# Linear attention and a mixture of experts in one kernel: the queries' sums by head move from TensorE and spreading transfers to ScalarE and VectorE

## The chip, the cores and the metric

The kernel runs on one core of a Trainium2 chip. A core has TensorE (matrix products into PSUM), VectorE, ScalarE and GpSimd for work on tiles of 128 partitions, and queues that start DMA transfers (SP's, ScalarE's and GpSimd's). The time is that of the whole program on the device in microseconds, and is given as the median of several runs. All numbers are in fp32; most products are made as three products of a high and a low part.

## The reference

```
qkv = x @ wqkv                                   # S = 2048 tokens, D = 512; 32 heads of 16
phi = lambda t: where(t > 0, t + 1, exp(t)) + 1e-6
pq, pk = phi(q), phi(k)
kv  = einsum("bhsd,bhse->bhde", pk, v)
z   = einsum("bhsd->bhd", pk)                    # sum of the keys over all tokens, by head
num = einsum("bhqd,bhde->bhqe", pq, kv)
den = einsum("bhqd,bhd->bhq", pq, z)[..., None] + 1e-6
a   = (num / den) @ wo
b   = sum over 8 experts: softmax weight * (silu(x @ w1[e]) @ w2[e])     # F = 1792
g   = sigmoid((x * gate_w).sum(-1))
out = g * a + (1 - g) * b
```

What matters here is `den`: for each token and each of the 32 heads, the sum over the head's 16 features of query times `z`. The kernel divides the query by `den` and multiplies it by the gate `g` before the product with the folded matrix of `kv` and `wo`.

## The kernel before

**Staging.** A first stage (`keys`) makes the keys' features and their sums: `pks` is a tile whose sum over partitions is `z`. The second stage (`experts`) is one long loop over ticks, `for u in range(LAG + NTICK)`, with an order written out by hand. In each tick TensorE does six products "up" (`up`, `product`: hidden layers of a group of two blocks of F, by Strassen's seven products, into PSUM banks a, b and c) and six products "down" (`tick`: the second layer into four banks `p`, of the pool `dn`). A part is 49 ticks, seven phases P1, P7, P2, P4, P6, P5, P3 of seven ticks; it is one expert and one half of the tokens. The attention is two more parts of 14 ticks each, `A[0]` and `A[1]`. While the tick's products run, `other()` gives ScalarE and VectorE work for later ticks: `prep` splits weights into a high part (`o`, ScalarE) and a low part (`o`, VectorE), `high` and `low_h` do the same for hidden values (`ho`), `differ` forms differences of `s` tiles. At the end of a phase `evict` empties the `p` banks: in P2 VectorE multiplies the bank by the expert's weights (`finish`, tile `c`), then ScalarE copies `keep` (`k`) into the bank.

**The queries' sums.** The queries' features lie in DRAM (`pqd`) as four blocks of 128 features by 512 tokens for each of four token blocks i. `m.beside` names the four parts beside which they are worked on: the first two experts of the second half, and two experts after `A[0]`. Step s of query i stands in tick t0 + s of its part.

- In stage two's start, `normaliser` makes on TensorE, with 16 products of 32x32 against a tile of ones, the vector z for all features in 32 equal columns, masks it by head on VectorE (`maskh`) and stores it in `zcd`.
- `queries_load` (s = -3) loads the masked z (`Q.z`) once for two queries, and the four blocks `Q.d`, over SP's queue. All of them lie in two large buffers (tag `rm`), named `az` and `pq` in the profile.
- `queries_first`, s = 0 to 3: ScalarE adds EPS to the four blocks. `queries_last`, s = 3: TensorE makes `dn`, four fp32 products of the blocks with the masked z, in one bank of pool `a`: the sums by head. s = 4: ScalarE copies `dn` to `r`, and the gate's row is loaded over all partitions (`rg`). s = 5 to 8: VectorE takes the reciprocal, a quarter at a time. s = 9: VectorE multiplies by the gate, and GpSimd's queue stores 8 heads of each block in `rd`. s = 10: it loads them back, each head's row spread over the 16 partitions of its features (`az<-rd`). s = 15 to 18: VectorE multiplies the blocks by them, SP's queue stores them in `pqd`, and the fourth block is spread.
- `load_query` reads `pqd` for the attention's parts, 100 ticks and more later.

The engines take their instructions in order, and so do the queues; semaphores hold an instruction until its inputs are there and its buffer is free.

Of the kernel before, what the change touches and what calls it, by code (L numbers as in the profile page):

```python
# [16 lines left out]
P = 128  # L17
# [26 lines left out]
@with_exitstack  # L44
def gated_mix_kernel(ctx: ExitStack, tc: tile.TileContext, xT, x, wk, wv, wqkv_q, wo, wm, out):
    nc = tc.nc
    PS = bass.MemoryType.PSUM

    const = ctx.enter_context(tc.tile_pool(name="const", bufs=1))
    xpool = ctx.enter_context(tc.tile_pool(name="xpool", bufs=14))  # L50
    w1p = ctx.enter_context(tc.tile_pool(name="w1p", bufs=1))
    psum = ctx.enter_context(tc.tile_pool(name="psum", bufs=1, space=PS))
    dram = ctx.enter_context(tc.tile_pool(name="dram", bufs=1, space=bass.MemoryType.DRAM))
    ctx.enter_context(tc.manual_schedule())

    m = SimpleNamespace(nc=nc, tc=tc, const=const, xpool=xpool, w1p=w1p, psum=psum, v=nc.vector,
                        xT=xT, x=x, wk=wk, wv=wv, wq=wqkv_q, wo=wo, wm=wm, out=out)

    def mm3(ps, wh, wlo, xh, xl, start, stop):
        nc.tensor.matmul(ps, wh, xh, start=start, stop=False, skip_group_check=True)  # L60
        nc.tensor.matmul(ps, wh, xl, start=False, stop=False, skip_group_check=True)  # L61
        nc.tensor.matmul(ps, wlo, xh, start=False, stop=stop, skip_group_check=True)  # L62

    def act_copy(dst, src, scale=1.0, bias=0.0):
        nc.scalar.activation(dst, src, AF.Copy, scale=scale, bias=bias)  # L65

    def ps_tile(name, tag, bufs=None):
        return psum.tile([P, TB], F32, name=name, tag=tag, bufs=bufs or {"a": 2, "b": 1, "c": 1, "dn": 4}[tag])

    m.mm3, m.act_copy, m.ps_tile = mm3, act_copy, ps_tile  # L70


    def phi_first(dst, src):
        nc.scalar.activation(dst, src, AF.Exp)
        nc.scalar.activation(src, src, AF.Relu)

    def phi_last(dst, src):
        nc.vector.scalar_tensor_tensor(dst, dst, 1.0, src, op0=ALU.min, op1=ALU.add)

    def phi(dst, src):  # L80
        phi_first(dst, src)
        phi_last(dst, src)

    def eps_high(h, d):
        act_copy(h, d, bias=EPS)

    def eps_low(lo, d, h):
        nc.vector.scalar_tensor_tensor(lo, d, EPS, f32(h), op0=ALU.add, op1=ALU.subtract)

    m.phi, m.phi_first, m.phi_last, m.eps_high, m.eps_low = phi, phi_first, phi_last, eps_high, eps_low  # L90
    m.ident = const.tile([P, P], F32, name="ident")


    def x_tile(name, tag="x"):
        return xpool.tile([P, 2, TB], F32R, name=name, tag=tag, bufs=14 if tag == "x" else 2)

    m.x_tile = x_tile
    m.XO = [[None] * 7, [None] * 7]
    m.xstash = dram.tile([7, 2, P, 2 * TB], F32, name="xstash")
    m.w2stash = [dram.tile([P, 2, D], F32, name=f"w2stash{i}") for i in range(7 * (E * NPAIR + 2) // 2)]  # L100
    m.wgtd = dram.tile([E + 1, S], F32, name="wgtd")
    m.acct = dram.tile([2, 2, KT, P, TB], F32, name="acct")
    m.pqd = dram.tile([2, 2, KT, P, TB], F32, name="pqd")
    m.wpd = [dram.tile([P, D], F32, name=f"wpd{c}") for c in range(KT)]
    m.zcd = dram.tile([P, KT * NH], F32, name="zcd")
    m.rd = dram.tile([2, 2, NH, TB], F32, name="rd")

    X = [[SimpleNamespace(e=e, h=h, n=NPAIR) for e in range(E)] for h in range(2)]  # L110
    A = m.A = [SimpleNamespace(e=E, h=h, n=2) for h in range(2)]
    M = E // 2

    m.parts = [*X[0], *X[1][:M], A[0], *X[1][M:], A[1]]
    at = 0
    for part in m.parts:
        part.t0, at = at, at + 7 * part.n
    m.NTICK = at
    m.groups = [(part, q) for part in (A[0], *X[0], *X[1][:M], A[1], *X[1][M:]) for q in range(part.n)]
    m.NG = len(m.groups)  # L120
    for part in m.parts:
        part.gs = [g for g, (p, _) in enumerate(m.groups) if p is part]
    m.G1 = X[1][0].gs[0]

    m.beside = [*X[1][:2], *X[1][M:M + 2]]

    misc = ExitStack()
    m.misc = misc.enter_context(tc.tile_pool(name="misc", bufs=1, side="right"))


    def pad(pool):
        nc.gpsimd.memset(pool.tile([P, 24], F32, name="pad", tag="pad", bufs=1), 0.0)

    m.pad = pad
    weights(m)
    keys(m)
    experts(m, misc)


# [186 lines left out]
def keys(m):  # L326
# [31 lines left out]
        return X[tb, k // 2][c][:, k % 2, lo:hi]  # L358

    mask = m.mask = misc.tile([P, P], F32, name="mask")  # L360
    maskh = m.maskh = misc.tile([P, KT, NH], F32, name="maskh")
    pks = m.pks = misc.tile([P, D], F32, name="pks")
    ones = m.ones = misc.tile([P, NH], F32, name="ones")
    lg = m.lg = misc.tile([P, NT, NL], F32, name="lg")
# [83 lines left out]
    def bands(t):  # L448
        if t == 5:
            band(mask.rearrange("p (b e) -> p b e", e=DH), [[-DH, P // DH], [0, DH]], 1)  # L450
        elif t == 6:
            band(maskh, [[P, KT], [-DH, NH]], 1)

    pk = {}

# [130 lines left out]
def experts(m, misc):  # L586
# [335 lines left out]


    def normaliser():
        ps = ps_tile("z", "dn")[:, :KT * NH]
        for c in range(KT):
            for a in range(QT):
                nc.tensor.matmul(ps[a * SQ:(a + 1) * SQ, c * NH:(c + 1) * NH],
                                 m.pks[:, c * P + a * SQ:c * P + (a + 1) * SQ], m.ones, start=(c == 0), stop=True,
                                 skip_group_check=True)  # L930
        zf = r_tile("zf")[:, :KT * NH].rearrange("p (c f) -> p c f", c=KT)
        v.scalar_tensor_tensor(zf, ps.rearrange("p (c f) -> p c f", c=KT), S * EPS, m.maskh, op0=ALU.add, op1=ALU.mult)
        nc.sync.dma_start(m.zcd, zf.rearrange("p c f -> p (c f)"))

    def gates(step):
        g = m.lg[:, :, :E]
# [36 lines left out]

    Q = SimpleNamespace()

    def queries_load(i):
        if i % 2 == 0:
            az = m.raw_tile(f"az{i}")
            Q.z = az[:, :KT * NH].rearrange("p (c f) -> p c f", c=KT)
            Q.by = [az[:, KT * NH + c * TB:KT * NH + (c + 1) * TB] for c in (0, 1, 2, 0)]  # L980
            nc.sync.dma_start(az[:, :KT * NH], m.zcd)
        Q.d = m.raw_tile(f"pq{i}").rearrange("p (c t) -> p c t", c=KT)
        for c in range(KT):
            nc.sync.dma_start(Q.d[:, c], m.pqd[i // 2, i % 2, c])

    def queries_first(i, s):
        h, j = divmod(i, 2)

        def spread(c):
            heads = m.rd[h, j, c * P // DH:(c + 1) * P // DH]  # L990
            nc.gpsimd.dma_start(Q.by[c], heads[:, None, :].to_broadcast([P // DH, DH, TB]))

        if 0 <= s < KT:
            act_copy(Q.d[:, s], Q.d[:, s], bias=EPS)
        elif s == 4:
            r = Q.r = out_tile(f"r{i}")
            Q.gate = out_tile(f"rg{i}")
            at = (2 * h + j) * TB
            nc.sync.dma_start(Q.gate, m.wgtd[E:E + 1, at:at + TB].to_broadcast([P, TB]))
            act_copy(r, Q.ps, bias=EPS)  # L1000
        if 5 <= s < 9:
            r = Q.r[:, (s - 5) * P:(s - 4) * P]
            v.reciprocal(r, r)
        elif s == 9:
            v.tensor_mul(Q.r, Q.r, Q.gate)
            for c in range(KT):
                n = P // DH
                at = c * (NH + n)
                nc.gpsimd.dma_start(m.rd[h, j, c * n:(c + 1) * n], Q.r[at:at + n])
        elif s == 10:  # L1010
            for c in range(KT - 1):
                spread(c)
        if 15 <= s < 15 + KT:
            d = Q.d[:, s - 15]
            v.tensor_mul(d, d, Q.by[s - 15])
            nc.sync.dma_start(m.pqd[h, j, s - 15], d)
            if s == 15:
                spread(KT - 1)

    def queries_last(i, s):  # L1020

        if s == KT - 1:
            Q.ps = ps_tile(f"dn{i}", "a")
            for c in range(KT):
                nc.tensor.matmul(Q.ps[c * NH:(c + 1) * NH, :], Q.z[:, c], Q.d[:, c], start=True, stop=True)


    def load_query(part, i):
# [104 lines left out]
    for u in range(LAG + NTICK):  # L1133
# [2 lines left out]
        g, k = divmod(u, 7)  # L1136


        query = [(i, n - part.t0) for i, part in enumerate(m.beside) if -3 <= n - part.t0 < 20]

        def mid():
            if n >= 0:
                tick(n)
            for i, s in query:
                queries_last(i, s)


        def spare(i, name):
# [7 lines left out]
        def other():  # L1156
# [15 lines left out]
            for i, s in query:  # L1172
                if s == -3:
                    queries_load(i)
                queries_first(i, s)
            q, s = divmod(u - 7 * WP, 21)
            if 0 <= q < 2 and s == 0:
                m.load_wp(q)
# [100 lines left out]
```

## Time and profile before

| | |
|---|---|
| median of 3 runs | 2330.51 us (2329.56 to 2331.95) |
| the profiled run, its time | 2328.57 us |
| its span, first to last instruction | 2326.5 us |
| granted TensorE clock, mean | 1.000 |
| DMA | 517.53 MB, 222 GB/s over the span |

In the profile an instruction is named by the line of the kernel, the engine, the operation, and the tiles it writes and reads (`out<-in`). "Idle before" is the time in which the engine did nothing ahead of an instruction, and behind the arrow stands what ended it. L60 to L62 are the three products of `mm3`, L65 is `act_copy`, L768 `low_h`, L207 a low half of `prep`, L817 the product in `finish`, L823 its transfer to `acct`, L793 the load of the second layer's weights, `w`. A matmul's length in the timeline overlaps the next one's; the distance of the starts is its share of TensorE. An fp32 product appears as two passes, so four `dn` products are eight rows.

### The profile page before, as it was taken

How to read it: one execution, taken by the hardware profiler on the slowest of the kernel's cores; microseconds unless marked ns; L12 is line 12 of the kernel's file. 1: busy time of each engine (PE TensorE's matmuls, PEld its weight loads, DVE VectorE, ACT ScalarE, POOL GpSimd, SP SyncE). 2: the span in 40 equal slices, each digit the busy share in tenths (PEclk: the TensorE clock that was granted, in tenths of full speed). 3: DMA queues.
4: the chain of work that ended last, by engine and by line, in shares of the span. 5: the costliest groups of instructions: out<-in, count | busy, mean ns of one | idle time of the engine just before them, and what ended most of it. 6: DMA issues, size and time to landing. Idle time of an engine off the chain costs nothing.

```text
span 2326.5 us, 31686 instructions
## 1 busy us (share of the span) xinstructions
PE 2319.4 (100%) x10584; PEld 1919.2 (82%) x10584; DVE 1813.3 (78%) x3088; ACT 1403.8 (60%) x2643; POOL 170.5 (7%) x241
## 2 busy tenths in 40 slices
PE   9999999999999999999999999999999999999999
PEld 8878888888888888888888888888888888888887
DVE  6799888888888888888677768776777676777777
ACT  6687666666666666666555555555565555555553
POOL 1101000000000000000001001000011100100101
PEclk9999999999999999999999999999999999999999
DMA  7899888988888898888845555664556656666568
GB/s 232 237 300 293 269 278 255 287 260 263 270 270 276 256 293 255 265 270 259 289 140 177 169 178 173 177 189 144 161 167 187 200 152 183 186 162 176 162 212 225
DMA packets 325619, 517.53 MB, mean 222 GB/s; under 512 B 51328, under 2 KB 220560, under 8 KB 325072
## 3 DMA queue, kind: packets, MB, share of 16 engines
q1 hardware_dynamic: 294720, 463.91, 60.4%
q0 software_dynamic: 26080, 50.69, 11.4%
q8 instruction: 83, 1.36, 0.2%
q10 hardware_dynamic: 4656, 0.92, 0.2%
q14 instruction: 80, 0.66, 0.1%
HBM read 347.75 MB, written 163.45 MB: 220 GB/s over the span
## 4 chain that ended last, share of the span: by engine, by line
PE 98%; DMA 1%; ACT 1%; DVE 0%; issue 0%; SPq 0%
PE p L60 16%; PE p L61 16%; PE p L62 16%; PE a L60 9%; PE a L61 9%; PE a L62 9%; PE c L61 4%; PE c L62 4%; PE c L60 4%; PE b L61 2%; PE b L60 2%; PE b L62 2%; PE g L459 2%; PE y L60 1%; PE y L62 1%; PE y L61 1%
## 5 line engine op out<-in xcount | busy, mean ns | idle before, releaser
L60 PE MATMUL p<-ho,w 128*128 128x512 f32 x1616 | 629.2, 389 | 0.1
L61 PE MATMUL p<-ho,w 128*128 128x512 f32 x1616 | 628.7, 389 | 0.0
L62 PE MATMUL p<-ho,w 128*128 128x512 f32 x1616 | 628.7, 389 | 0.0
L768 DVE TENSOR_TENSOR ho<-s,ho 128x512 fp32r<-128x512 f32 x784 | 536.7, 685 | 41.1 <-ACT ho L65 38.4
L65 ACT ACTIVATE ho<-s 128x512 fp32r<-128x512 f32 x784 | 480.9, 621 | 12.8 <-PE p L62 12.4
L60 PEld LDWEIGHTS p<-ho,w 128*128 128x128 f32 x1616 | 303.4, 188 | 65.2 <-ACT p L65 1.2
L62 PEld LDWEIGHTS p<-ho,w 128*128 128x128 f32 x1616 | 303.2, 188 | 63.0
L61 PEld LDWEIGHTS p<-ho,w 128*128 128x128 f32 x1616 | 303.3, 188 | 62.6
L65 ACT ACTIVATE o<-rs 128x512 fp32r<-128x512 f32 x224 | 129.2, 577 | 206.3 <-PE c L62 113.8
L65 ACT ACTIVATE o<-rm 128x512 fp32r<-128x512 f32 x240 | 138.4, 577 | 137.1 <-PE a L62 66.5
L698 DVE TENSOR_TENSOR s<-c,s 128x512 f32<-128x512 f32 x116 | 80.1, 691 | 156.4 <-PE c L62 148.2
L65 ACT ACTIVATE ws<-rm 128x256 fp32r<-128x256 f32 (+1 forms) x204 | 115.2, 572 | 54.5 <-DMA w2stash<-ws 46.8
L627 ACT ACTIVATE s<-s 128x512 f32<-128x512 f32 x224 | 138.4, 618 | 6.5 <-DVE s L704 4.0
L627 ACT ACTIVATE s<-b 128x512 f32<-128x512 f32 x112 | 67.0, 599 | 103.7 <-PE b L62 91.5
L704 DVE TENSOR_TENSOR s<-a,s 128x512 f32<-128x512 f32 x116 | 80.1, 690 | 63.0 <-PE a L62 62.7
L65 ACT ACTIVATE s<-a 128x512 f32<-128x512 f32 x116 | 69.2, 597 | 91.4 <-PE a L62 91.3
L207 DVE TENSOR_TENSOR o<-rm,o 128x512 fp32r<-128x512 f32 x180 | 123.1, 684 | 1.3 <-ACT o L65 1.2
L207 DVE TENSOR_TENSOR o<-rs,o 128x512 fp32r<-128x512 f32 x168 | 114.5, 681 | 8.6 <-ACT o L65 8.6
L221 DVE TENSOR_TENSOR ws<-rm,ws 128x512 fp32r<-128x512 f32 x155 | 106.1, 685 | 17.2 <-ACT ws L65 16.7
L65 ACT ACTIVATE b<-a 128x512 f32<-128x512 f32 x116 | 67.2, 579 | 65.3 <-PE a L62 65.2
L65 ACT ACTIVATE s<-c 128x512 f32<-128x512 f32 x116 | 69.0, 594 | 25.6 <-PE c L62 25.6
L823 POOL DMA_DIRECT2D acct<-c x30 | 26.3, 878 | 693.2 <-DVE c L817 526.5
(330 smaller groups left out, 4499.4 us busy)
## 6 DMA issues: line engine op xcount, KB each, us to landing
w<-w2stash SPq DMA_DIRECT2D x403, 512.0 KB, 4.3
w2stash<-ws SPq DMA_DIRECT2D x359, 256.0 KB, 4.7
rm<-wm SPq DMA_DIRECT2D x228, 256.0 KB, 5.3
rs<-wm SPq DMA_DIRECT2D x108, 256.0 KB, 4.1
wb<-wgtd SPq DMA_DIRECT2D x16, 512.0 KB, 4.8
acct<-c POOLq DMA_DIRECT2D x30, 256.0 KB, 6.2
acct<-d POOLq DMA_DIRECT2D x30, 256.0 KB, 5.8
acct<-k POOLq DMA_DIRECT2D x30, 256.0 KB, 5.7
```

The lines of the kernel that those rows point to most:

```text
L60: nc.tensor.matmul(ps, wh, xh, start=start, stop=False, skip_group_check=True)
L61: nc.tensor.matmul(ps, wh, xl, start=False, stop=False, skip_group_check=True)
L62: nc.tensor.matmul(ps, wlo, xh, start=False, stop=stop, skip_group_check=True)
L65: nc.scalar.activation(dst, src, AF.Copy, scale=scale, bias=bias)
L207: v.tensor_sub(two(o, 1), src, f32(two(o, 0)))
L221: v.tensor_sub(two(w, 1), src, f32(two(w, 0)))
L459: nc.tensor.matmul(ps, xk((0, 0, 1)[j], tb, k, tt * P, (tt + 1) * P), gw[g][:, (0, 1, 0)[j], k, :], start=(k == 0 and j == 0), stop=(k == ...
L627: nc.scalar.activation(dst, src, AF.Silu)
L698: v.tensor_add(sn[g, 2], bank[g, "c"], sn[g, 2])
L704: v.tensor_add(sn[g, 3], bank[g, "a"], sn[g, 3])
L768: v.tensor_sub(h[1], s, f32(h[0]))
L823: nc.gpsimd.dma_start(m.acct[part.h, j, dt], s, accum_op=ALU.add)
```

## The change

The tile `maskh` and the DRAM tiles `zcd` and `rd` go. `normaliser` makes two columns in place of 32 and leaves z in SBUF as one value for each feature (`m.z`). A query becomes 22 steps in place of 20, none of them on TensorE:

- for each block c, s = 3c: ScalarE adds EPS and then makes a copy scaled by z, feature by feature. s = 3c + 1: VectorE transposes it in squares of 32 (inside each square tokens lie on partitions then, and the features of two heads side by side). s = 3c + 2: VectorE sums each run of 16, which gives 32 values on each partition.
- s = 12: VectorE adds EPS and takes the reciprocal of all 128 values of a partition. s = 13: it multiplies by the gate, which `queries_load` has fetched over GpSimd's queue, in four transfers of single elements, so that tokens lie on partitions.
- for each block c, s = 14 + 2c: VectorE transposes the values back, reading each 16 times. s = 15 + 2c: it multiplies the block and SP's queue stores it.

The working tiles `Q.t` and `Q.sq` lie in the same buffer `az`; the two small output tiles that a query took (`r`, `rg`) are no longer taken.

```diff
     def normaliser():
-        ps = ps_tile("z", "dn")[:, :KT * NH]
+        ps = ps_tile("z", "dn")[:, :2 * KT]
         for c in range(KT):
             for a in range(QT):
-                nc.tensor.matmul(ps[a * SQ:(a + 1) * SQ, c * NH:(c + 1) * NH],
-                                 m.pks[:, c * P + a * SQ:c * P + (a + 1) * SQ], m.ones, start=(c == 0), stop=True,
-                                 skip_group_check=True)
-        zf = r_tile("zf")[:, :KT * NH].rearrange("p (c f) -> p c f", c=KT)
-        v.scalar_tensor_tensor(zf, ps.rearrange("p (c f) -> p c f", c=KT), S * EPS, m.maskh, op0=ALU.add, op1=ALU.mult)
-        nc.sync.dma_start(m.zcd, zf.rearrange("p c f -> p (c f)"))
+                nc.tensor.matmul(ps[a * SQ:(a + 1) * SQ, 2 * c:2 * c + 2],
+                                 m.pks[:, c * P + a * SQ:c * P + (a + 1) * SQ], m.ones[:, :2], start=(c == 0),
+                                 stop=True, skip_group_check=True)
+        m.z = hp.tile([P, SQ], F32, name="z", tag="z", bufs=1)
+        v.tensor_scalar(m.z[:, :KT], ps.rearrange("p (c f) -> p c f", f=2)[:, :, 0], S * EPS, None, op0=ALU.add)
...
+    QS = 3 * KT + 2 + 2 * KT
+
     def queries_load(i):
         if i % 2 == 0:
             az = m.raw_tile(f"az{i}")
-            Q.z = az[:, :KT * NH].rearrange("p (c f) -> p c f", c=KT)
-            Q.by = [az[:, KT * NH + c * TB:KT * NH + (c + 1) * TB] for c in (0, 1, 2, 0)]
-            nc.sync.dma_start(az[:, :KT * NH], m.zcd)
+            *Q.t, Q.sq, rest = (az[:, c * TB:(c + 1) * TB] for c in range(KT))
+            Q.r, Q.gate = rest[:, :P], rest[:, P:P + TB // SQ]
         Q.d = m.raw_tile(f"pq{i}").rearrange("p (c t) -> p c t", c=KT)
         for c in range(KT):
             nc.sync.dma_start(Q.d[:, c], m.pqd[i // 2, i % 2, c])
+        gate = m.wgtd[E, i * TB:(i + 1) * TB].rearrange("(b i) -> i b", i=SQ)
+        for a in range(QT):
+            nc.gpsimd.dma_start(Q.gate[a * SQ:(a + 1) * SQ], gate)
+
+    def queries(i, s):
         h, j = divmod(i, 2)
...
+        def heads(c):
+            return Q.r[:, c * SQ:(c + 1) * SQ]
+
+        if 0 <= s < 3 * KT:
+            c, step = divmod(s, 3)
+            if step == 0:
+                act_copy(Q.d[:, c], Q.d[:, c], bias=EPS)
+                nc.scalar.activation(Q.t[c % 2], Q.d[:, c], AF.Copy, scale=m.z[:, c:c + 1])
+            elif step == 1:
+                v.transpose(Q.sq, Q.t[c % 2])
+            else:
+                v.tensor_reduce(heads(c), Q.sq.rearrange("p (n f) -> p n f", f=DH), axis=AX.X, op=ALU.add)
+        elif s == 3 * KT:
+            v.tensor_scalar(Q.r, Q.r, EPS, None, op0=ALU.add)
+            v.reciprocal(Q.r, Q.r)
+        elif s == 3 * KT + 1:
+            r = Q.r.rearrange("p (c b h) -> p c b h", c=KT, h=SQ // DH)
+            v.tensor_mul(r, r, Q.gate[:, None, :, None].to_broadcast([P, KT, TB // SQ, SQ // DH]))
+        elif s < QS:
+            c, step = divmod(s - 3 * KT - 2, 2)
+            if step == 0:
+                v.transpose(Q.t[c % 2], heads(c)[:, :, None].to_broadcast([P, SQ, DH]))
+            else:
+                d = Q.d[:, c]
+                v.tensor_mul(d, d, Q.t[c % 2])
+                nc.sync.dma_start(m.pqd[h, j, c], d)
...
-        query = [(i, n - part.t0) for i, part in enumerate(m.beside) if -3 <= n - part.t0 < 20]
+        query = [(i, n - part.t0) for i, part in enumerate(m.beside) if -3 <= n - part.t0 < QS]
...
-            for i, s in query:
-                queries_last(i, s)
...
-                queries_first(i, s)
+                if s >= 0:
+                    queries(i, s)
```

The functions `queries_first` and `queries_last` go, whose text stands above with the kernel before.

More of the change, by code (lines that the diff above doesn't have):

```diff
@@ L104, in gated_mix_kernel @@
     m.wpd = [dram.tile([P, D], F32, name=f"wpd{c}") for c in range(KT)]
-    m.zcd = dram.tile([P, KT * NH], F32, name="zcd")
-    m.rd = dram.tile([2, 2, NH, TB], F32, name="rd")
     X = [[SimpleNamespace(e=e, h=h, n=NPAIR) for e in range(E)] for h in range(2)]
@@ L360, in keys @@
     mask = m.mask = misc.tile([P, P], F32, name="mask")
-    maskh = m.maskh = misc.tile([P, KT, NH], F32, name="maskh")
     pks = m.pks = misc.tile([P, D], F32, name="pks")
@@ L450, in bands @@
             band(mask.rearrange("p (b e) -> p b e", e=DH), [[-DH, P // DH], [0, DH]], 1)
-        elif t == 6:
-            band(maskh, [[P, KT], [-DH, NH]], 1)
     pk = {}
@@ L984, in queries_load @@
             nc.sync.dma_start(Q.d[:, c], m.pqd[i // 2, i % 2, c])
-    def queries_first(i, s):
+        gate = m.wgtd[E, i * TB:(i + 1) * TB].rearrange("(b i) -> i b", i=SQ)
+        for a in range(QT):
+            nc.gpsimd.dma_start(Q.gate[a * SQ:(a + 1) * SQ], gate)
+    def queries(i, s):
         h, j = divmod(i, 2)
[L989 to L1025, printed above, removed]
+        def heads(c):
[23 more added lines that the diff above has]
+                nc.sync.dma_start(m.pqd[h, j, c], d)
```

## The prediction

> **What bounds the kernel now.** I read the page first: the busy shares and the chain of waits.
>
> ```profile
> span 2326.5 us, 31686 instructions
> PE 2319.4 (100%) x10584; PEld 1919.2 (82%) x10584; DVE 1813.3 (78%) x3088; ACT 1403.8 (60%) x2643; POOL 170.5 (7%) x241
> PE 98%; DMA 1%; ACT 1%; DVE 0%; issue 0%; SPq 0%
> ```
>
> TensorE is busy for 2319.4 of 2326.5 us, and 98% of the chain that ended last is its own matmuls, one behind the other. So a matmul taken away shortens the kernel by its slot, as long as nobody makes TensorE wait instead. The products that the change removes are the `dn` group. I then read TensorE's timeline at the first and the last query (columns: start, length, engine, line, operation, tiles, shape, count).
>
> ```profile
> 1257.03 0.39 PE L61 MATMUL p<-ho,w 128*128 128x512 f32 x1
> 1257.26 0.39 PE L62 MATMUL p<-ho,w 128*128 128x512 f32 x1
> 1257.57 1.52 PE L1025 MATMUL dn<-pq,az 128*32 128x512 f32 x8
> 1259.02 0.50 PE L60 MATMUL a<-n5h,o 128*128 128x512 f32 x1
> 1259.36 0.40 PE L61 MATMUL a<-n5l,o 128*128 128x512 f32 x1
> ...
> 1966.75 0.39 PE L62 MATMUL p<-ho,w 128*128 128x512 f32 x1
> 1967.07 1.52 PE L1025 MATMUL dn<-pq,az 128*32 128x512 f32 x8
> 1968.52 0.50 PE L60 MATMUL a<-n5h,o 128*128 128x512 f32 x1
> 1968.86 0.40 PE L61 MATMUL a<-n5l,o 128*128 128x512 f32 x1
> ```
>
> An ordinary matmul starts 0.23 us after the one before (1257.03 to 1257.26). The lengths of 0.39 overlap and don't count; starts do. Around `dn` the starts go from 1257.26 to 1259.36, 2.10 us, where two ordinary steps take 0.46. The detour costs 1.64 us, in the last query the same (1966.75 to 1968.86, 2.11). It holds the eight passes and a slower step into and out of them.
>
> Third, what VectorE and ScalarE have left in the 22 ticks that a query will take. A tick is one step of the hand-written order, 12 matmuls of 0.227, 2.72 us. These are the four stretches, step 0 to step 21 (columns: length, then busy us and count of TensorE, weight loads, VectorE, ScalarE, GpSimd, clock, DMA share, GB/s).
>
> ```profile
> 1246.60:1308.10 61.50, 61.50 (x273) 49.76 (x272) 47.84 (x83) 35.71 (x67) 5.34 (x9) 1.00 0.57 183
> 1381.55:1443.05 61.50, 61.50 (x273) 49.76 (x272) 47.84 (x83) 35.70 (x67) 6.30 (x10) 1.00 0.59 181
> 1821.15:1882.65 61.50, 61.50 (x273) 49.76 (x272) 46.89 (x81) 36.42 (x68) 7.20 (x11) 1.00 0.63 193
> 1956.10:2017.60 61.50, 61.50 (x273) 49.76 (x272) 47.84 (x83) 35.71 (x67) 7.19 (x11) 1.00 0.61 184
> ```
>
> TensorE has no idle time there and the clock is 1.00. VectorE is idle for 61.50 - 47.84 = 13.7 us, ScalarE for 25.8. That idle time is the cover for all that the change adds.
>
> **The change part by part.** *TensorE, queries.* Four groups of `dn` leave: 4 x 1.64 = 6.6 us off the path. Nothing is added to TensorE there.
>
> *TensorE, normaliser.* The 16 products stay but write 2 columns in place of 32.
>
> ```profile
> 107.78 0.39 PE L62 MATMUL a<-x00h,o 128*128 128x512 f32 x1
> 108.10 0.46 PE L928 MATMUL z<-ones,pks 128*32 128x32 f32 x32
> 108.49 0.50 PE L60 MATMUL a<-t6h,o 128*128 128x512 f32 x1
> ```
>
> The group holds TensorE from 108.10 to 108.49. It stays in the narrow form, so the slow steps around it stay. Between 0 (the 32 passes cost their issue, not their columns) and 0.39 us can go; I take 0.1, near nothing, because the columns are the smaller part of such short passes.
>
> *VectorE.* Means of one instruction, from the groups by form:
>
> ```profile
> L1003 DVE RECIPROCAL r<-r 128x128 f32<-128x128 f32 x16 | 15.1, 945 | 0.0
> L1015 DVE TENSOR_TENSOR pq<-pq,az 128x512 f32<-128x512 f32 x16 | 10.9, 683 | 0.0
> L1049 DVE STREAM_TRANSPOSE row<-acc 128x512 f32<-128x512 f32 x8 | 5.6, 704 | 0.0
> L957 DVE TENSOR_TENSOR gates<-gates 128x128 f32<-128x128 f32 x1 | 0.3, 295 | 0.0
> L951 DVE TENSOR_REDUCE gates<-gates 128x16 f32<-128x128 f32 x1 | 0.2, 229 | 0.0
> L949 DVE TENSOR_SCALAR gates<-gates 128x16 f32<-128x16 f32 x1 | 0.2, 168 | 0.0
> L65 ACT ACTIVATE pq<-pq 128x512 f32<-128x512 f32 x16 | 9.9, 621 | 0.0
> ```
>
> A query now has four reciprocals, one product with the gate row (512 wide as L1015) and four last products: 4 x 0.945 + 5 x 0.683 = 7.2 us. It will have eight transposes (5.6), four reductions, one addition and one reciprocal over 128 elements, one product over 128 (0.3) and the four last products (2.7). The reduction of 512 elements isn't in the trace: a quarter of its elements took 0.229, and the costliest one-input row here is 0.945. I take 0.69, that of other instructions over 512 elements. The addition is between 0.168 (16 wide) and 0.295; I take 0.2. Sum: 5.6 + 2.8 + 0.2 + 0.9 + 0.3 + 2.7 = 12.5, so 5.3 us more than now in each query (3.5 and 6.3 with the two ends of the reduction). The transposes back read each value 16 times in a row; the row at 0.704 reads a plain tile, and twice that is my upper bound, 2.8 more. The window gets 1.6 shorter, so of 13.7 idle about 6.8 remain. I cost VectorE at nothing; with the cover gone it is 5.3 us a query.
>
> [...]
>
> *Where it is tightest.* In steps 14 to 21 a transpose or a last product falls in each tick, where now products fall in 15 to 18 alone. Steps 19 and 20 also empty the banks of phase P2, VectorE first and ScalarE behind it, before TensorE writes these banks again:
>
> ```profile
> 1302.88 0.69 DVE L817 TENSOR_TENSOR c<-p,wb 128x512 f32<-128x512 f32 x1 [1.31 <-PE p L62]
> 1303.60 0.60 ACT L65 ACTIVATE p<-k 128x512 f32<-128x512 f32 x1 [3.13 <-DVE c L817]
> 1305.89 0.68 DVE L817 TENSOR_TENSOR c<-p,wb 128x512 f32<-128x512 f32 x1
> 1306.61 0.60 ACT L65 ACTIVATE p<-k 128x512 f32<-128x512 f32 x1 [1.06 <-DVE c L817]
> 1306.76 0.39 PE L60 MATMUL p<-ho,w 128*128 128x512 f32 x1
> 1309.47 0.39 PE L60 MATMUL p<-ho,w 128*128 128x512 f32 x1
> ```
>
> The first eviction had 1.31 us of idle time before it, which takes the new product of step 19. The first bank is free at 1304.20 and written at 1306.76. The second eviction stands behind the transpose of step 20, some 0.7 us later than 1305.89; ScalarE's copy then ends near 1307.9, and TensorE writes that bank at 1309.47. About 1.6 us remain. Behind a late eviction stand the low halves `ho` and `o`, which are made ticks before their products. So no stall, cost 0.
>
> *ScalarE.* Four scaled copies come (4 x 0.62), one eviction of `dn` goes: about 1.9 us more a query, in 25.8 idle. They stand in steps 0, 3, 6, 9 ahead of bank copies. I take that late copies still end within the tick that follows. VectorE's transpose waits for a copy issued a tick earlier; behind it wait only low halves.
>
> *Queues.* SP loses the loads of `zcd` and of the gate row; its four stores move to steps 15, 17, 19, 21, each behind its product. GpSimd's queue loses eight transfers a query and gets four, three steps ahead of the query, in pieces of 4 bytes, 512 each.
>
> ```profile
> L991 POOL DMA_DIRECT2D az<-rd x16 | 9.7, 612 | 48.6 <-DVE pq L1015 44.0 <-DMA rd<-r 3.8 <-issue 0.4
> L1009 POOL DMA_DIRECT2D rd<-r x16 | 8.3, 523 | 197.4 <-DVE r L1005 197.2 <-issue 0.2
> 1241.36 0.32 SPq L793 DMA_DIRECT2D w<-w2stash  x1
> w<-w2stash SPq DMA_DIRECT2D x403, 512.0 KB, 4.3
> 1253.40 0.39 PE L60 MATMUL p<-ho,w 128*128 128x512 f32 x1
> ```
>
> 8 rows cost GpSimd 0.523, 128 rows 0.612: under 0.001 a piece. 512 pieces make an estimate of 0.9; if each costs more, a few us on an engine that is 7% busy, with only `acct` transfers behind it. The gates are needed by step 13, 16 ticks or 43 us later. The danger is to others: weights issued at 1241.36 land some 4.3 later, near 1245.7, for products at 1253.40. Some 7.7 us of delay would be hidden. The queue is also freed of GpSimd's waits (197.2 and 44.0 us), which cost nothing now.
>
> **Sum.** 6.6 + 0.1 = 6.7 us off the profiled execution's span, 2326.5 to 2319.8. The profiled run took 2328.57, 2.1 around the span, and lies 1.9 under the median of the runs, 2330.51. The step is the same against each: 2330.5 - 6.7 = 2323.8 us, 0.29% less.
>
> **The rivals.** *A: part of it is given back.* TensorE runs into another limit in the same ticks, because 1.6 us of delay was shifted and not removed: an eviction or a low half that was just in time is now late. For it: the second bank of P2 keeps 1.6 us, and VectorE's share in a query goes to some 89% (53.1 of 59.9). Against it: no TensorE row in the four stretches waits. A stall of 0.6 to 1.6 us in each query leaves 2326.2 to 2330.2; I would say 2328.
>
> *B: slower, VectorE becomes the bound in a query's second half.* One mechanism: the transposes of repeated values. In the last eight ticks there is room for one transpose more every second tick at 0.7, not at 1.4. From about 1.1 us each (the 1.6 spare spread over the four that stand ahead of it, if nothing of them is absorbed) the second bank is late, and everything in order behind it. If all 5.3 us plus the 2.8 show up on TensorE, each query costs 8.1 - 1.64 = 6.5, in all 26: 2356; with half of that 2343. For it: no row shows that form. Against it: 6.8 us remain on the whole query.
>
> *C: the pieces of 4 bytes hold up the weight loads.* If 2048 pieces delay a load by over 7.7 us, each query loses what exceeds that: at 12 us of delay 4.3 - 1.64, in all 10.6: 2341. [...] No row of this trace has a fetch of that form.
>
> **How the numbers follow.** Forecast 0.70, A 0.20, B 0.06, C 0.04. About 0.2%, 4.7 us, is what a measurement of this kernel can tell from no change, so the line is 2325.8. The forecast's own range is 2321.5 (0.3 more from the normaliser, and 2 us of spread, since the runs before lie 2.4 apart) to 2325.8. A reaches to 2330; that much of A leaves less than 2 in 10 outside. B and C stay outside. Faster 0.71 (a little of A's near end, less the forecast's far end), same 0.19, slower 0.10.
>
> **What would show it.** In the changed profile: `dn` gone and a step of 0.23 from `p` to `a` at step 3 of each query; no wait of TensorE on VectorE or ScalarE in the four stretches; VectorE some 5 us busier in each, with transposes near 0.7 and reductions below 0.95; `c<-p` of step 20 within 1.6 us of its old place; the fetch of gates landed before step 13. I am wrong if a step of TensorE over 0.3 us stands in these stretches, and by B if it is at P2's second bank, by C if a product waits for `w`.

## The result and the profile after

| | before | after |
|---|---|---|
| median of 4 runs each | 2330.03 us (2329.06 to 2331.95) | 2355.07 us (2354.21 to 2359.38) |
| the profiled run, its time and span | 2328.57, span 2326.5 | 2354.21, span 2352.5 |
| ratio after / before | | 1.0109, 95% interval 1.0097 to 1.0121 |

The kernel became 25 us slower, where 6.7 us faster was predicted. The head of the page of after (span, busy time and count by engine, chain of waits by engine):

```profile
span 2352.5 us, 31622 instructions
PE 2345.5 (100%) x10552; PEld 1918.1 (82%) x10552; DVE 1831.6 (78%) x3128; ACT 1410.9 (60%) x2655; POOL 161.0 (7%) x222
PE 99%; DMA 0%; ACT 0%; DVE 0%; SPq 0%; issue 0%
```

TensorE has 32 rows fewer (10552 for 10584) and is busy 26.1 us longer. The chain of waits is still TensorE's own, with even less of other engines in it than before. So nobody makes TensorE wait; its own work takes longer. How much longer one matmul takes is read from windows in which TensorE has no idle time: length over count is the mean step from start to start. The windows of before, then of after (columns as in the prediction: length, then busy us and count of TensorE, weight loads, VectorE, ScalarE, GpSimd, clock, DMA share, GB/s):

```profile
130.00:170.00 40.00, 40.00 (x178) 33.11 (x177) 38.74 (x64) 33.12 (x64) 0.00 (x0) 1.00 0.91 287
212.00:300.00 88.00, 88.00 (x390) 72.88 (x389) 76.92 (x129) 57.44 (x110) 4.84 (x10) 1.00 0.84 271
300.00:1240.00 940.00, 940.00 (x4148) 778.35 (x4148) 772.97 (x1291) 591.84 (x1115) 46.67 (x54) 1.00 0.83 260
```

```profile
130.00:170.00 40.00, 40.00 (x178) 33.14 (x177) 38.80 (x65) 33.31 (x64) 0.00 (x0) 1.00 0.91 289
212.00:300.00 88.00, 88.00 (x384) 71.78 (x383) 75.10 (x126) 57.19 (x109) 5.43 (x12) 1.00 0.83 266
300.00:1240.00 940.00, 940.00 (x4085) 766.50 (x4084) 764.68 (x1275) 584.42 (x1101) 44.37 (x52) 1.00 0.82 257
```

Between 130 and 170 us the two are alike, 178 matmuls in 40 us. From 212 us on the step is 940 / 4148 = 0.2266 us before and 940 / 4085 = 0.2301 after, at the same granted clock, 1.00. No query runs in these windows: the first one comes behind 1240 us. The loss is spread over the second stage (from 1450 to 1800 us there are 1546 matmuls before and 1522 after), and it begins between 170 and 212 us, where the first down products `p<-ho,w` stand. Six down products of one tick of before, and of one of after, in TensorE's timeline, from the first of the six to the product behind them (columns: start, length; starts count):

```profile
600.60 0.39 PE L60 MATMUL p<-ho,w 128*128 128x512 f32 x1
600.83 0.39 PE L61 MATMUL p<-ho,w 128*128 128x512 f32 x1
...
601.96 0.39 PE L60 MATMUL b<-x01h,o 128*128 128x512 f32 x1
```

```profile
601.72 0.40 PE L60 MATMUL p<-ho,w 128*128 128x512 f32 x1
601.95 0.39 PE L61 MATMUL p<-ho,w 128*128 128x512 f32 x1
...
603.11 0.39 PE L60 MATMUL a<-t6h,o 128*128 128x512 f32 x1
```

Six products took 601.96 - 600.60 = 1.36 us before and take 603.11 - 601.72 = 1.39 after. No step stands out, which is why a search for stalls finds nothing: the longest step of after between 1240 and 2060 us, where the queries run, is 0.238 us. The products write and read the same tiles, in the same order, in both.

What did change for them is where a tile lies. The new tile `m.z` is 128 bytes on each partition and is taken from the pool of the hidden values (`hp`), ahead of the five `ho` tiles. As the pools lay the tiles out, `ho` begins at byte 195328 of a partition after, and at 195200 before. Modulo 256 these are 0 and 128. All other operands of the second stage's up and down products (the `x` and difference tiles, `o`, `w`) begin at 128 modulo 256 in both kernels. The products `p` have `ho` as the moving operand (the 128x512 of the rows above) and `w` as the weights that are loaded (128x128, 0.19 us in a load's row).

Not every hidden value lies in these five tiles. `high` puts one in six (`n % 6 == 5`) into the pool of the `x` tiles, where it begins at 128 in both kernels. That makes a comparison inside the kernel after. Here are two of its ticks, each from its first product to the first of the next tick. By the order of the hidden values in the program the first tick reads `ho` at 0, the second at 128:

```profile
300.69 0.40 PE L60 MATMUL p<-ho,w 128*128 128x512 f32 x1
...
303.46 0.40 PE L60 MATMUL p<-ho,w 128*128 128x512 f32 x1
...
328.34 0.39 PE L60 MATMUL p<-ho,w 128*128 128x512 f32 x1
...
331.06 0.40 PE L60 MATMUL p<-ho,w 128*128 128x512 f32 x1
```

Twelve steps take 303.46 - 300.69 = 2.77 us with `ho` at 0, and 331.06 - 328.34 = 2.72 us with `ho` at 128, as much as a tick takes in the kernel before. Over the window from 300 to 1240 us the mean step is 0.2306 us in the 252 ticks whose `ho` lies at 0 throughout, and 0.2267 in the 24 whose `ho` lies at 128 throughout.

### The profile page after: what moved, and what is told of

Its sections match the earlier page's. It is cut to its first block, busy times and chain, and to the rows that moved or that the text cites. A ratio compares the mean times of both kernels' runs of the same rounds, so it can differ in the third digit from the quotient of the medians.

```text
span 2352.5 us, 31622 instructions
## 1 busy us (share of the span) xinstructions
PE 2345.5 (100%) x10552; PEld 1918.1 (82%) x10552; DVE 1831.6 (78%) x3128; ACT 1410.9 (60%) x2655; POOL 161.0 (7%) x222
## 3 DMA queue, kind: packets, MB, share of 16 engines
q8 instruction: 83, 1.36, 0.2%
## 4 chain that ended last, share of the span: by engine, by line
PE 99%; DMA 0%; ACT 0%; DVE 0%; SPq 0%; issue 0%
PE p L62 16%; PE p L60 16%; PE p L61 16%; PE a L61 9%; PE a L60 9%; PE a L62 9%; PE c L61 4%; PE c L60 4%; PE c L62 4%; PE b L61 2%; PE b L60 2%; PE b L62 2%; PE g L454 2%; PE y L60 1%; PE y L62 1%; PE y L61 1%
## 5 line engine op out<-in xcount | busy, mean ns | idle before, releaser
L62 PE MATMUL p<-ho,w 128*128 128x512 f32 x1616 | 637.1, 394 | 0.0
L60 PE MATMUL p<-ho,w 128*128 128x512 f32 x1616 | 635.7, 393 | 0.0
L61 PE MATMUL p<-ho,w 128*128 128x512 f32 x1616 | 633.3, 392 | 0.0
```

## The experiments

Theory 1 said that the place of `ho` makes the steps longer. Its rivals were the changed rotation of the `r` buffers (theory 2) and the added work on VectorE and ScalarE (theory 3). Four kernels tried that; the kernel before, run beside them, took 2329.38 us. Each ratio is to the kernel before, with its 95% interval.

**e1_z_256: the kernel after, with another 128 bytes.**

```
-        m.z = hp.tile([P, SQ], F32, name="z", tag="z", bufs=1)
+        m.z = hp.tile([P, 2 * SQ], F32, name="z", tag="z", bufs=1)
```

> The changed kernel with the tile z 256 bytes a partition in place of 128, so that the five ho tiles behind it start 256 and not 128 bytes above their old addresses; nothing else differs. Theory 1 (place of ho: a shift by 128 bytes slows the products that read ho): the steps of TensorE are 0.227 us again, the time is 2330 - 6.6 = 2323.5 us, ratio 0.997. Theory 2 (the order of the r buffers, which moved by one when zf went): still near 2355. Theory 3 (the added work on VectorE and ScalarE): still near 2355.

Measured: 2321.92 us, ratio 0.9971 (0.9959 to 0.9982). Its span on the page:

```profile
span 2320.3 us, 31622 instructions
PE 2313.3 (100%) x10552; PEld 1919.7 (83%) x10552; DVE 1832.3 (79%) x3128; ACT 1410.2 (61%) x2655; POOL 161.6 (7%) x222
```

The window that held 4148 matmuls before and 4085 after:

```profile
300.00:1240.00 940.00, 940.00 (x4149) 778.61 (x4148) 774.72 (x1292) 591.34 (x1116) 48.85 (x58) 1.00 0.84 260
```

With the change's whole work in it and 128 unused bytes more, the step is 0.2266 again and the kernel is faster than before. Of the two kernels and all variants, it is with f1 (below) the fastest. The size of an unread remainder of a buffer is worth 2352.5 - 2320.3 = 32.2 us of span. Theories 2 and 3 fall: the rotation and the added work are those of the kernel after.

**e2_before_128: the kernel before, with a tile of 128 bytes that nobody reads.**

```
         nc.sync.dma_start(m.zcd, zf.rearrange("p c f -> p (c f)"))
+        nc.gpsimd.memset(hp.tile([P, SQ], F32, name="zpad", tag="z", bufs=1), 0.0)
```

> The kernel before with one unused tile of 128 bytes a partition at the place where the changed kernel has z, cleared once by GpSimd; the queries' work is the old one. Theory 1 (place of ho): some 32 us slower, 2330 + 32 = 2362 us, steps of TensorE near 0.230 from 180 us on. Theory 2 and theory 3: 2330 us, nothing moved but addresses.

Measured: 2362.94 us, ratio 1.0144 (1.013 to 1.0157), with none of the change in it. The same window:

```profile
300.00:1240.00 940.00, 940.00 (x4086) 766.44 (x4084) 765.11 (x1277) 585.21 (x1104) 45.05 (x52) 1.00 0.83 257
```

4086 matmuls, where after has 4085. The loss needs the shift and nothing else.

**e3_w_128 and e4_z_64: which places are bad?** In e3 `w` is shifted with `ho`, in e4 `ho` is shifted by 64 bytes in place of 128. e3:

```
-                m.pad(m.w2p)
+                nc.gpsimd.memset(m.w2p.tile([P, 56], F32, name="pad", tag="pad", bufs=1), 0.0)
```

and e4:

```
-        m.z = hp.tile([P, SQ], F32, name="z", tag="z", bufs=1)
+        m.z = hp.tile([P, SQ // 2], F32, name="z", tag="z", bufs=1)
```

> The changed kernel with the pad behind the w2 tiles made 128 bytes larger, so that w moves by 128 bytes too and has the same distance from ho as before, modulo 256. Theory 1a (what counts is the distance of ho and w, the two operands that TensorE reads at once): 2323.5 us. Theory 1b (what counts is the place of ho alone): still near 2355 us, or slower if w has to lie right by itself. Theory 2 and theory 3: near 2355.

> The changed kernel with z 64 bytes a partition, so that ho starts 64 bytes above its old address. Theory 1: if only the 128 bytes' bit of the address counts, 2323.5 us; if ho has to lie on the old place modulo 256, 2350 us or more. Theory 2 and theory 3: near 2355.

Measured: e3 2344.45 us, ratio 1.0062 (1.0047 to 1.0077); e4 2361.03 us, ratio 1.0136 (1.0123 to 1.015). The same window of e3, then of e4:

```profile
300.00:1240.00 940.00, 940.00 (x4105) 772.86 (x4105) 767.76 (x1281) 586.65 (x1106) 45.23 (x53) 1.00 0.83 258
```

```profile
300.00:1240.00 940.00, 940.00 (x4071) 763.98 (x4070) 763.24 (x1273) 582.46 (x1100) 44.38 (x52) 1.00 0.83 257
```

Neither "the distance of `ho` and `w` alone" (e3 would be near 0.2267, and is at 0.2290) nor "the place of `ho` alone" (e3 would be as after) holds. In e3 `w` and the five `ho` tiles lie at 0 modulo 256, and `x` and `o`, the operands of the up products, still at 128; the two groups alternate six by six. (The hidden values in the pool of the `x` tiles stay at 128 there, apart from `w`. Without them, in the 252 ticks of the window whose `ho` lies at 0 throughout, the step is 0.2283.) Of the two outcomes that theory 1 left open for e4 the second came: `ho` 64 bytes off its old place is no better than 128 bytes off. That left two forms of the theory: operands that follow one another must lie alike, wherever that is (1c), or 128 modulo 256 is a fast place as such (1d). Three more runs took them apart (the kernel before, run beside them: 2329.58 us).

**f1_all_128: the kernel after, with all operands at 0 modulo 256.**

```
     m.ident = const.tile([P, P], F32, name="ident")
+    nc.gpsimd.memset(const.tile([P, SQ], F32, name="cpad"), 0.0)
...
-    def pad(pool):
-        nc.gpsimd.memset(pool.tile([P, 24], F32, name="pad", tag="pad", bufs=1), 0.0)
+    def pad(pool, n=24):
+        nc.gpsimd.memset(pool.tile([P, n], F32, name="pad", tag="pad", bufs=1), 0.0)
...
-                m.pad(m.w2p)
+                m.pad(m.w2p, 56)
...
-        m.z = hp.tile([P, SQ], F32, name="z", tag="z", bufs=1)
+        m.z = hp.tile([P, 2 * SQ], F32, name="z", tag="z", bufs=1)
```

> The kernel after, with every operand of the matmuls moved by 128 bytes: a tile of 128 bytes behind `ident` moves x, o and the rest of the left side, the padding of w's pool goes from 24 to 56 floats, and z takes 256 bytes, so that ho moves by 128 + 128 too. All of x, o, ho and w then begin at a multiple of 256 bytes, where in the kernel before they begin 128 behind one. Theory 1c (operands that lie alike modulo 256 are fast, wherever that is): steps of 0.2267, 2322 us. Theory 1d (128 behind a multiple of 256 is the fast place, a multiple of 256 a slow one): every step at least as slow as in e3_w_128, 2344 us or more.

Measured: 2322.9 us, ratio 0.9971 (0.9961 to 0.998), and in the window:

```profile
300.00:1240.00 940.00, 940.00 (x4148) 778.60 (x4148) 773.82 (x1293) 592.14 (x1116) 48.73 (x58) 1.00 0.84 260
```

0 is as good as 128, as long as everything lies there. Theory 1d falls. In this kernel `ho` lies at 0 modulo 256, as in the slow kernel after.

**f2_before_w: the kernel before, with `w` alone moved by 128 bytes** (the larger padding of e3, in the kernel before).

> The kernel before, in which only w is moved by 128 bytes (padding of its pool 56 floats in place of 24), and ho, x and o stay. Theory 1c: ho and w lie differently modulo 256, as in the kernel after, so the p products slow down: 2345 to 2365 us. Theory 1b (only the place of the moving operand ho counts): 2330 us, as before.

Measured: 2365.06 us, ratio 1.0153 (1.0138 to 1.0168); in the window:

```profile
300.00:1240.00 940.00, 940.00 (x4079) 767.07 (x4078) 763.62 (x1274) 583.69 (x1103) 44.91 (x52) 1.00 0.83 257
```

Moving the weights against `ho` costs 35 us, as moving `ho` against the weights did (33.6 in e2). Theory 1b falls.

**f3_places: the step by itself.** A kernel of its own, which ran once, with only this loop (the rest of each call's arguments cut) for 16 pairs of places, and then the same beside 500 copies each on VectorE and ScalarE. The granted clock is 1.00 in all stretches read below:

```
# six(ps, m, w, c), 16 times for each pair
xh, xl = m[:, :TB], m[:, TB:]
for k in range(2):
    lo = (c % 2 * 4 + k * 2) * P
    wh, wl = w[:, lo:lo + P], w[:, lo + P:lo + 2 * P]
    nc.tensor.matmul(ps, wh, xh, ...)
    nc.tensor.matmul(ps, wh, xl, ...)
    nc.tensor.matmul(ps, wl, xh, ...)
```

> Leaves the whole computation out and measures the step by itself: groups of 96 matmuls of 128x128 by 128x512 in fp32r, one behind another, for each of 16 pairs of places modulo 256 of the moving tile (m: a 128, b 192, c 0, d 64) and of the weights (w: the same letters); first with the other engines idle (banks p), then beside copies of VectorE and ScalarE (banks q); then groups of six that alternate between two pairs (banks u and v). Theory 1c: 0.2267 us where both lie alike, longer where they differ, with the other engines idle too. Theory 1d: 0.2267 at 128 for both alone. If it is the other engines' accesses that meet the reads of TensorE, the steps are all 0.2267 or less in the first part and differ in the second.

TensorE's timeline at the first matmul of each group of 96 (the second letter is the place: a 128, b 192, c 0, d 64; banks p with the other engines idle, banks q beside the copies):

```profile
79.29 0.39 PE L57 MATMUL pa<-ma,wa 128*128 128x512 f32 x1
...
101.05 0.40 PE L57 MATMUL pb<-ma,wb 128*128 128x512 f32 x1
...
123.45 0.39 PE L57 MATMUL pa<-ma,wc 128*128 128x512 f32 x1
...
145.76 0.39 PE L57 MATMUL pb<-ma,wd 128*128 128x512 f32 x1
...
167.74 0.39 PE L57 MATMUL pa<-mb,wa 128*128 128x512 f32 x1
...
189.73 0.40 PE L57 MATMUL pb<-mb,wb 128*128 128x512 f32 x1
...
433.15 0.39 PE L57 MATMUL qa<-ma,wa 128*128 128x512 f32 x1
...
454.95 0.40 PE L57 MATMUL qb<-ma,wb 128*128 128x512 f32 x1
...
477.35 0.39 PE L57 MATMUL qa<-ma,wc 128*128 128x512 f32 x1
...
499.66 0.39 PE L57 MATMUL qb<-ma,wd 128*128 128x512 f32 x1
...
521.64 0.39 PE L57 MATMUL qa<-mb,wa 128*128 128x512 f32 x1
```

The distance of two starts over 96 is the step:

| weights ahead of the moving tile by (modulo 256) | pair | step, others idle | step, beside copies |
|---|---|---|---|
| 0 | ma,wa | (101.05 - 79.29) / 96 = 0.2267 us | (454.95 - 433.15) / 96 = 0.2271 |
| 64 | ma,wb | (123.45 - 101.05) / 96 = 0.2333 | (477.35 - 454.95) / 96 = 0.2333 |
| 128 | ma,wc | (145.76 - 123.45) / 96 = 0.2324 | (499.66 - 477.35) / 96 = 0.2324 |
| 192 | ma,wd | (167.74 - 145.76) / 96 = 0.2290 | (521.64 - 499.66) / 96 = 0.2290 |

The pair mb,wa has the same distance as ma,wd, 192, and takes (189.73 - 167.74) / 96 = 0.2291. The other eleven pairs follow the same rule in the trace to within 0.0002 us: only the distance modulo 256 counts. The steps differ in the first part, where the other engines did nothing, as they do beside the copies. So it isn't their accesses that make the difference.

The last part of this kernel rebuilt the ticks of three kernels: six products with operands at 128 and six with another pair, in turn. Their first starts, and the start of the third part's 190th matmul:

```profile
787.05 0.39 PE L57 MATMUL u<-ma,wa 128*128 128x512 f32 x1
...
831.30 0.39 PE L57 MATMUL u<-ma,wa 128*128 128x512 f32 x1
...
875.15 0.39 PE L57 MATMUL u<-ma,wa 128*128 128x512 f32 x1
...
918.73 0.39 PE L57 MATMUL v<-ma,wc 128*128 128x512 f32 x1
```

Over 192 matmuls each, ma,wa in turn with mc,wa (the tick of after) has a step of (831.30 - 787.05) / 192 = 0.2305, where after has 0.2301 (0.2306 in its ticks with `ho` at 0); in turn with mc,wc (the tick of e3) (875.15 - 831.30) / 192 = 0.2284, where e3 has 0.2290 (0.2283 in its ticks with `ho` at 0). In turn with ma,wc (the tick of f2) it is (918.73 - 875.15) / 189 = 0.2306, where f2 has 940 / 4079 = 0.2304. No other work is in this kernel, so the places alone give the slowdown of these three, to within 0.0002 us a step. With mc,wc the loss stands at the changes from one place to the other: the step into a new group of six takes 0.232 us and the next one 0.231, the other four 0.227 (means over the repeats).

The tick of e4 (`ho` at 192, `w` at 128) was not rebuilt, and the table alone doesn't give it: half of the steps at 0.2290 and half at 0.2267 would be 0.2279, and e4 has 940 / 4071 = 0.2309. In e4 even the up products, whose own operands lie alike, take 0.2312 in the mean of the window. Why this alternation costs more stays open.

## Why the prediction was wrong

**The step that failed is in the sum: that nothing changes on TensorE but the listed work.** The prediction says "Nothing is added to TensorE there" and adds up 6.6 and 0.1 us and nothing else, with the ordinary step of 0.23 us taken as given for both kernels. That step is a property of where the operands lie, and the diff moved one of them: `m.z = hp.tile([P, SQ], ...)` stands in the change, and the prediction prices the work that uses the new tile and nowhere what the tile pushes aside. The missing term is 0.2301 - 0.2266 = 0.0035 us for each of some 9,350 matmuls from 200 us to the end (2152 us over 0.2301), 32.7 us; e1 against after measured 32.2. With it the sum is 2326.5 - 6.7 + 32.7 = 2352.5, and the profile has 2352.5; that it meets to the tenth is luck, since 6.7 and 32.7 are each 0.5 more than the 6.2 and 32.2 that e1 shows. None of the rivals was this: A, B and C all look for a step over 0.3 us, and the sign by which I would be wrong, "a step of TensorE over 0.3 us stands in these stretches", does not show it either.

**Everything else can be judged in e1_z_256,** the change without the shift, which took 2321.92 us where 2323.8 was predicted, inside the forecast's own range of 2321.5 to 2325.8; the span went down by 2326.5 - 2320.3 = 6.2 us for a predicted 6.7.

*TensorE, queries: right.* At step 3 of the first query the `dn` group's place is one ordinary step. The kernel after, TensorE's timeline:

```profile
1274.08 0.39 PE L62 MATMUL p<-ho,w 128*128 128x512 f32 x1
1274.31 0.39 PE L60 MATMUL a<-n5h,o 128*128 128x512 f32 x1
```

*TensorE, normaliser: right in kind, 0.1 was too much.* From the product ahead of the group to the one behind it, 108.49 - 107.78 = 0.71 us before, and in e1 109.13 - 108.45 = 0.68:

```profile
108.45 0.39 PE L62 MATMUL a<-x00h,o 128*128 128x512 f32 x1
108.76 0.43 PE L923 MATMUL z<-ones,pks 128*32 128x2 f32 x32
109.13 0.50 PE L60 MATMUL a<-t6h,o 128*128 128x512 f32 x1
```

*VectorE, ScalarE and queues: right.* The instructions on `az` in the kernel after (shortest/median/longest ns; first and last start):

```profile
L982 POOL DMA_DIRECT2D az<-wgtd x16: 648/733/999, 1247.2 to 1964.2; - x16
L994 ACT ACTIVATE az<-pq,z x16: 722/725/727, 1264.6 to 2004.5; 128x512 f32<-128x512 f32 x16
L996 DVE STREAM_TRANSPOSE az<-az x16: 705/711/716, 1266.4 to 2006.0; 128x512 f32<-128x512 f32 x16
L998 DVE TENSOR_REDUCE az<-az x16: 678/680/684, 1268.4 to 2010.2; 128x32 f32<-128x512 f32 x16
L1008 DVE STREAM_TRANSPOSE az<-az x16: 703/704/707, 1302.5 to 2037.1; 128x512 f32<-128x512 f32 x16
L1000 DVE TENSOR_SCALAR az<-az x4: 221/222/223, 1297.8 to 2013.2; 128x128 f32<-128x128 f32 x4
...
DMA to landing us min/median/max: 2.6/5.1/7.7
```

The reduction takes 0.680 (taken: 0.69), the transpose 0.711 and with repeated values 0.704 (0.704, and at most twice that), the addition 0.222 (0.2). The reduction is no slower here than its neighbours, since a query's last product, also over 512 elements, takes 0.684. The scaled copy takes 0.725 where I took 0.62 from the copy with a constant: a term missized by 0.1 each, hidden in ScalarE's idle time. The gates' fetch costs GpSimd 0.73 each (estimate 0.9) and lands within 7.7 us of its issue, far ahead of step 13. So rivals B and C had no ground. The cover, in the query's 22 ticks of e1:

```profile
1246.00:1305.84 59.84, 59.84 (x265) 49.57 (x264) 51.11 (x91) 37.24 (x69) 4.30 (x6) 1.00 0.53 161
```

VectorE has 59.84 - 51.11 = 8.7 us left (6.8 was worked out), and TensorE is busy throughout. Over the whole kernel VectorE is busy 1832.3 - 1813.3 = 19.0 us longer, 4.75 a query, where 5.3 was predicted.

*The tightest place: right.* The second bank of P2 in the first query of e1 (L812 is the product in `finish` there), ScalarE's copy behind the eviction and TensorE's next product into the banks:

```profile
1305.62 0.65 DVE L812 TENSOR_TENSOR c<-p,wb 128x512 f32<-128x512 f32 x1
1306.31 0.60 ACT L65 ACTIVATE p<-k 128x512 f32<-128x512 f32 x1 [1.66 <-DVE c L812]
1308.58 0.39 PE L60 MATMUL p<-ho,w 128*128 128x512 f32 x1
```

The copy ends at 1306.91, 1.67 us ahead of the product; 1.6 was predicted. Nothing is given back (rival A): between 1240 and 2060 us, where all four queries run, no step of TensorE in e1 is longer than 0.227 us.

## What to carry to other kernels

A kernel whose engine is full of one instruction, here over 9,000 matmuls in a row, has that instruction's step as its largest term: before summing up what an edit adds and removes, see whether it moves an operand of that step, and a new tile ahead of others in their pool does. When the time changes and no wait appears, divide a long window by its count in both kernels; a step that is 1.5% longer everywhere can't be seen row by row. In this kernel, let all operands of the matmuls begin at the same byte modulo 256: here a tile of 256 bytes in place of 128 turned a loss of 1.1% into a gain of 0.3%.

## What the runs showed of the hardware

- The step of matmuls of 128x128 by 128x512 in fp32r, each with its weight load, depends on the distance of the weights' place from the moving tile's place in a partition, modulo 256 bytes: 0.2267 us at 0, 0.2333 at 64, 0.2324 at 128, 0.2290 at 192. It was measured at multiples of 64 bytes, for this shape and type alone.
- It isn't a conflict with VectorE or ScalarE: the steps are the same to within 0.0004 us with both idle and beside their copies (0.2333 both times at 64, 0.2267 and 0.2271 at 0). What in TensorE makes it so was not tried.
- The next weights are loaded while a matmul runs: in the kernel before, one of `w` runs for 0.19 us from 1261.20, between the starts of two products at 1261.19 and 1261.42. What such a load takes from the running matmul was not measured. The runs show a step that is shortest where both operands lie alike and otherwise up to 0.2333 / 0.2267 = 1.029 times as long; whether a read is held up then, or something else in TensorE, is not shown.
- A place counts across groups too. Six products at 0 in turn with six at 128, each six with both operands alike, have a step of 0.2284 us in f3 and 0.2283 in e3's ticks of that kind, against 0.2267. With `ho` at 192 in turn with 128 (e4) it is 0.2309, more than the distances of the single products give.
